# Second-block bursts: two attention groups at a time in four PSUM banks, with every engine in source order

## The chip, the cores and the metric

The kernel runs on one core of one Trainium2 chip. The metric is device time in microseconds (us) for one execution. Five engines work side by side: TensorE (PE in the profile; PEld is its weight loads), VectorE (DVE), ScalarE (ACT), GpSimd (POOL) and SyncE (SP), which here only issues DMAs.

## The reference

Sparse attention over 8 batches, 8 heads, 576 tokens and 64 columns a head, then a two-layer feed-forward with SiLU over all 4608 tokens:

```python
scores = scale * np.matmul(q, k.transpose(0, 1, 3, 2))
mask_local = (rel >= 0) & (rel < stride)                       # heads 0 to 3, stride 32
mask_strided = (rel >= 0) & (pos[None, :] % stride == pos[:, None] % stride)   # heads 4 to 7
scores = np.where(masks[None], scores, -1e9)
attn = softmax(scores)                                         # max taken off, sum + 1e-9
x = np.matmul(attn, v).transpose(0, 2, 1, 3).reshape(B * S, H * D)   # 4608 x 512
h = x @ w_in                                                   # 512 x 2048
g = h * (1.0 / (1.0 + np.exp(-h)))
out = g @ w_out                                                # 2048 x 512
```

## The kernel before

**Feed-forward.** The 4608 tokens are cut into nine blocks of 512 (`k` 0 to 8). A block runs through 16 chunks `fc` of 128 hidden columns. For each chunk `hidden` makes a 128x512 product in one PSUM bank of the ring `ps` (4 banks) with 12 matmuls. Weights and inputs are split into a high and a low part in fp32r, and three of the four products of the parts are kept. `silu` follows: `tanh` on ScalarE, then on VectorE `gate` (th), `g_high` (a cast to ghi) and `g_low` (a subtraction to glo). `output` adds the chunk to the four banks `po` of the block, again with 12 matmuls of 512 columns. In program order TensorE does `hidden(fc)` and then `output(fc-1)`, so that `silu(fc)` has one `output` to finish in. At a block's end `store` scales the four `po` banks on ScalarE and SP writes them out. In the last two chunks `x_high` (ScalarE) and `x_low` (VectorE) split the next block's inputs out of the attention result `xb`.

**Attention.** Each batch has six groups (`NG`), three of the local heads (12 tiles each) and three of the strided heads (8, 8 and 6 tiles), taken in turn: local, strided, local and so on. Group `c` of the list `groups` belongs to batch `c // 6`. The first two batches, and the first block with the loading of the weights, are laid out by a planner of its own (`steps.arrange()`), which also scores groups 12 and 13, takes their peaks, exponentials and sums, and scales them. From the second block on, attention is done in bursts between feed-forward chunks. One call `products(c)` is one burst: TensorE multiplies the weights of group `c` by its values (`values_by_halves`, in the left half of two `ps` banks) and scores group `c + 2` (`scores`, in the right half of the same banks). Then ScalarE copies the values into `xb` (`done_by_halves`; a strided group goes through `sort`), VectorE takes the masked scores' minima (`peak`, 6 instruction pairs for a local group, 8 or 6 for a strided one), ScalarE takes an exponential for each, VectorE divides (`total`, `scale`) and transposes by 32x32 blocks (`turn_by_blocks`: two wide transposes and four narrow ones). A matmul of a burst is plain fp32, and the trace records each as two.

`plan` puts six bursts into each of the blocks 1 to 6, after the chunks 0, 3, 5, 8, 11 and 13. Blocks 7 and 8 have none. One list `due` orders the loads on SP: keys and values of a group in turn. TensorE runs in program order throughout. The other engines do so only until the planner's end (`others.close()`); from there the compiler's scheduler orders them by its own cost model.

```python
    others.enter_context(tc.manual_schedule(engines=OTHERS))
```

Of the kernel before, what the change touches and what calls it, by code (L numbers as in the profile page):

```python
# [13 lines left out]
F32 = mybir.dt.float32  # L14
# [3 lines left out]
AF = mybir.ActivationFunctionType  # L18
# [31 lines left out]
KBUFS = 2  # L50
VBUFS = 2
# [34 lines left out]
NG = len(GROUPS)  # L86
# [112 lines left out]
def sparse_attention_ffn(ctx: ExitStack, tc: tile.TileContext, kqt, vt, w_in, w_out, out):  # L199
    nc = tc.nc  # L200
# [5 lines left out]
    ps = ctx.enter_context(tc.tile_pool(name="ps", bufs=8 - NTT, space=PSUM))  # L206
# [158 lines left out]
    class Attention:  # L365
# [36 lines left out]
        def peak(self):  # L402
            g = self.g
            s_ps = self.halves(self.pss)
            self.sm = att.tile([P, 512], F32, name="sm", bufs=3)
            self.s_sb = self.sm.rearrange("p (c h k) -> p c h k", h=2, k=KW)[:, : g.n]
            s_sb = self.s_sb
            sums = att.tile([P, 4, 4, 2], F32, name="sums", bufs=4)
            self.peaks, self.rsum = peaks, rsum = sums[:, 0, : g.n], sums[:, 1, : g.n]
            self.inv = rsum.unsqueeze(3).broadcast_to([P, g.n, 2, KW])  # L410
            for c in range(g.n):
                for h in range(2):

                    nc.vector.tensor_tensor_reduce(  # L414
                        out=s_sb[:, c, h], in0=s_ps[h][:, c], in1=masks[g.local, g.starts[c]][:, :KW],
                        scale=-SCALE, scalar=BIG, op0=ALU.add, op1=ALU.min,
                        accum_out=peaks[:, c, h : h + 1],
                    )
                    if not self.quick:
                        nc.scalar.activation(  # L420
                            out=s_sb[:, c, h], in_=s_sb[:, c, h], func=AF.Exp,
                            bias=peaks[:, c, h : h + 1], scale=-1.0,
                            accum_out=rsum[:, c, h : h + 1],
                        )

        def below(self):
            peaks = self.peaks.unsqueeze(3).broadcast_to([P, self.g.n, 2, KW])
# [132 lines left out]
    def new_x():  # L560
        return [[None] * NP for _ in range(2)]
# [9 lines left out]
    def x_high(k, x, cc, engine="ACT"):  # L571
        for half, name in zip(x, ("xhi", "xlo")):
            half[cc] = ffn.tile([P, T], F32R, name=name, bufs=XBUFS)
        for src, to in parts(k, cc):
            copy[engine](out=x[0][cc][:, to], in_=src)

    def x_low(k, x, cc):
        for src, to in parts(k, cc):
            nc.vector.tensor_sub(out=x[1][cc][:, to], in0=src, in1=x[0][cc][:, to].bitcast(F32))

    def hidden(fc, x, ccs, ph=None):

        if ph is None:
            ph = ps.tile([P, T], F32, name="ps")
        for cc in ccs:
            for n, (wi, xi) in enumerate(((0, 0), (0, 1), (1, 0))):
                nc.tensor.matmul(  # L587
                    ph, weight(0, wi, fc)[:, cc * P : (cc + 1) * P], x[xi][cc],
                    start=(cc, n) == (0, 0), stop=(cc, n) == (NP - 1, 2),
                )  # L590
        return ph
# [117 lines left out]
    x = new_x()  # L709
# [89 lines left out]
    x1 = new_x()  # L799
# [2 lines left out]
        x_steps(1, x1, cc, x_after + nexts, begin + pace * (NFC - 1))  # L802
    for step in steps.arrange():
        step.act()
    others.close()

    due = [(kind, j) for j in range(2 * NG, len(groups)) for kind in "kv"]
    due = [what for what in due if what not in (("k", 2 * NG), ("k", 2 * NG + 1))]
    scored, weighed = set(range(2 * NG + 2)), set(range(2 * NG))

    def load_due():

        while due:
            kind, j = due[0]
            bufs, load_one, read = (KBUFS, load_qk, scored) if kind == "k" else (
                VBUFS, load_v, weighed)
            if j - bufs not in read:
                return
            load_one(groups[j])
            due.pop(0)  # L820

    def products(c):

        banks = [ps.tile([P, 512], F32, name="ps") for _ in range(2)]
        value, later = groups[c], groups[c + 2] if c + 2 < len(groups) else None
        value.values_by_halves([bank[:, : P * 2] for bank in banks])
        weighed.add(c)
        if later:  # L830
            later.scores([bank[:, P * 2 :] for bank in banks])
            scored.add(c + 2)
        load_due()
        value.done_by_halves()
        if later:
            later.peak()
            later.total()
            later.scale()
            later.turn_by_blocks()

    plan = {}
    for c in range(2 * NG, len(groups)):
        b, at = divmod(c, NG)
        plan[b - 1, (0, 3, 5, 8, 11, 13)[at]] = c

    def between(k, fc):
        if (k, fc) in plan:
            products(plan[k, fc])

    for c in (2 * NG, 2 * NG + 1):  # L850
        groups[c].turn_by_blocks()
    load_due()
    lag = (0, NFC - 1, state["g", NFC - 1])
    po = state["po"]
    x = x1
    for k in range(1, NBLK):
        for fc in range(NFC):
            ph = hidden(fc, x, range(NP))
            new = (k, fc, silu(k, fc, ph))
            output(*lag, po)  # L860
            if fc == 0:
                store(k - 1, po)
                po = [ps_o.tile([P, DM], F32, name="po") for _ in range(NTT)]
            between(k, fc)
            lag = new
            if fc >= NFC - 2 and k + 1 < NBLK:
                if fc == NFC - 2:
                    x1 = new_x()
                for cc in range(NP // 2) if fc == NFC - 2 else range(NP // 2, NP):
                    x_high(k + 1, x1, cc)  # L870
                    x_low(k + 1, x1, cc)
                if fc == NFC - 1:
                    x = x1
    output(*lag, po)
    store(NBLK - 1, po)

# [67 lines left out]
```

## Time and profile before

| what | value |
|---|---|
| runs | 902.83 us median of 3 (901.41 to 903.88) |
| the profiled execution | 902.58 us, its span 900.8 us |
| busy shares | PE 98%, PEld 80%, DVE 56%, ACT 33%, POOL 2% |
| matmuls of 512 columns, recorded | 1728 for `hidden`, 1728 for `output` |
| data moved | 64.59 MB, 72 GB/s on average |

The span begins with the first instruction of the profiled execution and ends with its last. A busy PE in these rows is a modelled span: consecutive matmuls overlap in the records, so that the distance between starts tells their rate, not the duration that stands beside them. PEclk is the granted TensorE clock. In rows of the timeline the first number is the start in the span, the second the duration.

### The profile page before, as it was taken

How to read it: one execution, taken by the hardware profiler on the slowest of the kernel's cores; microseconds unless marked ns; L12 is line 12 of the kernel's file. 1: busy time of each engine (PE TensorE's matmuls, PEld its weight loads, DVE VectorE, ACT ScalarE, POOL GpSimd, SP SyncE). 2: the span in 40 equal slices, each digit the busy share in tenths (PEclk: the TensorE clock that was granted, in tenths of full speed). 3: DMA queues.
4: the chain of work that ended last, by engine and by line, in shares of the span. 5: the costliest groups of instructions: out<-in, count | busy, mean ns of one | idle time of the engine just before them, and what ended most of it. 6: DMA issues, size and time to landing. Idle time of an engine off the chain costs nothing.

```text
span 900.8 us, 17950 instructions
## 1 busy us (share of the span) xinstructions
PE 884.3 (98%) x7297; PEld 717.9 (80%) x7297; DVE 508.5 (56%) x1608; ACT 300.5 (33%) x899; POOL 19.9 (2%) x42
## 2 busy tenths in 40 slices
PE   8999998999999999999999999999999999999998
PEld 6777776788887888788878888887888888888886
DVE  6999678455565565646655565456464433333333
ACT  4768453322522333324332252324322221112111
POOL 5100000000000000000000000000000000000000
PEclk9999999999999999999999999999999999999999
DMA  8976542111311212212221131211300010001001
GB/s 259 312 228 191 167 123 87 47 52 40 115 35 37 71 36 91 60 33 75 84 66 34 50 110 30 60 49 50 100 19 10 1 47 1 1 0 47 1 1 47
DMA packets 37042, 64.59 MB, mean 72 GB/s; under 512 B 2912, under 2 KB 23776, under 8 KB 36960
## 3 DMA queue, kind: packets, MB, share of 16 engines
q1 hardware_dynamic: 36960, 63.45, 22.2%
q8 instruction: 57, 0.93, 0.4%
q14 instruction: 25, 0.20, 0.1%
HBM read 54.00 MB, written 9.44 MB: 70 GB/s over the span
## 4 chain that ended last, share of the span: by engine, by line
PE 76%; DVE 12%; ACT 6%; DMA 3%; SPq 1%; issue 1%; ACTq 0%; DVEq 0%
PE po L633 37%; PE ps L587 34%; ACT sm L420 3%; PE ps L502 3%; DVE pt L469 3%; PE ps L396 2%; DMA stage<-w_out 2%; DMA k<-kqt 1%; DVE th L601 1%; DVE glo L613 1%; DVE sm L444 1%; DVE pt L466 1%; DVE stage L293 1%; ACT xb L542 1%; DVE sm L414 1%
## 5 line engine op out<-in xcount | busy, mean ns | idle before, releaser
L587 PE MATMUL ps<-xhi,w 128*128 128x512 f32 x1152 | 386.2, 395 | 1.8 <-DVE th L601 1.3
L587 PEld LDWEIGHTS ps<-xhi,w 128*128 128x128 f32 x1152 | 216.1, 188 | 49.9 <-DVE th L601 1.5
L601 DVE SCALAR_TENSOR_TENSOR th<-th,ps 128x512 f32<-128x512 f32 (+1 forms) x147 | 99.2, 674 | 226.4 <-ACT th L597 225.5
L597 ACT ACTIVATE th<-ps 128x512 f32<-128x512 f32 (+1 forms) x147 | 86.3, 587 | 419.8 <-PE ps L587 417.1
L587 PE MATMUL ps<-xlo,w 128*128 128x512 f32 x576 | 224.3, 389 | 0.0
L633 PE MATMUL po<-w,ghi 128*128 128x512 f32 x504 | 156.8, 392 | 1.7 <-DVE ghi L609 1.7
L587 PEld LDWEIGHTS ps<-xlo,w 128*128 128x128 f32 x576 | 108.2, 188 | 21.3
L633 PEld LDWEIGHTS po<-w,ghi 128*128 128x128 f32 x504 | 95.2, 189 | 22.2 <-DVE ghi L609 2.1
L613 DVE TENSOR_TENSOR glo<-th,ghi 128x512 fp32r<-128x512 f32 (+1 forms) x147 | 100.1, 681 | 11.2 <-DVE ghi L609 0.5
L633 PE MATMUL po<-w,glo 128*128 128x512 f32 x252 | 99.8, 396 | 1.0 <-DVE glo L613 1.0
L633 PE MATMUL po<-stage,ghi 128*128 128x512 f32 x288 | 89.0, 390 | 0.0
L420 ACT ACTIVATE sm<-sm,sums 128x64 f32<-128x64 f32 x226 | 75.6, 337 | 2.9 <-DVE sums L414 2.3
L633 PE MATMUL po<-v,ghi 128*128 128x512 f32 x216 | 66.6, 390 | 0.0
L609 DVE CAST ghi<-th 128x512 fp32r<-128x512 f32 (+1 forms) x142 | 58.8, 414 | 9.4
L633 PEld LDWEIGHTS po<-stage,ghi 128*128 128x128 f32 x288 | 53.9, 188 | 11.2
L633 PEld LDWEIGHTS po<-w,glo 128*128 128x128 f32 x252 | 47.7, 189 | 14.2 <-DVE glo L613 4.4
L469 DVE STREAM_TRANSPOSE pt<-sm 32x192 f32<-32x192 f32 (+1 forms) x144 | 56.5, 392 | 2.7
L633 PE MATMUL po<-stage,glo 128*128 128x512 f32 x144 | 56.6, 393 | 0.5
L633 PEld LDWEIGHTS po<-v,ghi 128*128 128x128 f32 x216 | 40.5, 188 | 8.5
L633 PE MATMUL po<-k,ghi 128*128 128x512 f32 x144 | 44.3, 389 | 0.0
L414 DVE CUSTOM_DVE_ANT_0 sm<-ps,mask_strided 128x64 f32<-128x64 f32 x176 | 27.2, 220 | 28.3 <-ACT xb L542 28.1
L633 PE MATMUL po<-v,glo 128*128 128x512 f32 x108 | 42.1, 390 | 0.5 <-DVE glo L613 0.5
(84 smaller groups left out, 715.6 us busy)
## 6 DMA issues: line engine op xcount, KB each, us to landing
out<-stage SPq DMA_DIRECT2D x36, 256.0 KB, 2.1
v<-vt SPq DMA_DIRECT2D x21, 384.0 KB, 3.7
k<-kqt SPq DMA_DIRECT2D x14, 512.0 KB, 4.1
stage<-w_out SPq DMA_DIRECT2D x14, 512.0 KB, 4.6
stage<-w_in SPq DMA_DIRECT2D x12, 512.0 KB, 4.4
k<-kqt SPq DMA_DIRECT2D x14, 416.0 KB, 4.8
v<-vt SPq DMA_DIRECT2D x14, 256.0 KB, 2.9
k<-kqt SPq DMA_DIRECT2D x7, 448.0 KB, 4.4
```

The source lines that it names most:

```text
L293: nc.vector.scalar_tensor_tensor(out=upper, in0=upper, scalar=3, in1=lower, op0=ALU.logical_shift_left, op1=ALU.bitwise_or,)
L396: nc.tensor.matmul(self.pss[h][rows, c * KW : (c + 1) * KW], kbd[at, 1, g.q0[t] : g.q0[t] + g.rows], kbd[at, 0, g.k0[t] : g.k0[t] + KW], s ...
L414: nc.vector.tensor_tensor_reduce(out=s_sb[:, c, h], in0=s_ps[h][:, c], in1=masks[g.local, g.starts[c]][:, :KW], scale=-SCALE, scalar=BIG, ...
L420: nc.scalar.activation(out=s_sb[:, c, h], in_=s_sb[:, c, h], func=AF.Exp, bias=peaks[:, c, h : h + 1], scale=-1.0, accum_out=rsum[:, c, h ...
L469: nc.vector.transpose(out=pt[to, r % 2], in_=src[rows, 1 - r % 2])
L502: nc.tensor.matmul(self.pso[p][h * D : (h + 1) * D, i * size : (i + 1) * size], vbd[at, 2 * i + h], moved, start=True, stop=True,)
L587: nc.tensor.matmul(ph, weight(0, wi, fc)[:, cc * P : (cc + 1) * P], x[xi][cc], start=(cc, n) == (0, 0), stop=(cc, n) == (NP - 1, 2),)
L597: nc.scalar.activation(out=th[:, cols], in_=ph[:, cols], func=AF.Tanh, scale=0.5)
L601: nc.vector.scalar_tensor_tensor(out=th[:, cols], in0=th[:, cols], scalar=1.0, in1=ph[:, cols], op0=ALU.add, op1=ALU.mult,)
L609: copy[engine](out=g[0][:, cols], in_=th[:, cols])
L613: nc.vector.tensor_sub(out=g[1][:, cols], in0=th[:, cols], in1=g[0][:, cols].bitcast(F32))
L633: nc.tensor.matmul(po[tt], g[gi][:, cols], weight(1, wi, fc), start=fc == 0 and n == 0, stop=fc == NFC - 1 and n == 2,)
```

## The change

From the second block on, three bursts a block take the place of six, after the chunks 1, 6 and 11. A burst takes two groups, a local and a strided one, and so four `ps` banks, which is the whole ring. Within a burst TensorE scores the later local group first, then multiplies the values of the local and of the strided group, and scores the later strided group last. Right behind the burst comes the `output` of the chunk before it, so the next chunk has a `hidden` and no `output`, and two `hidden` follow each other.

The exponentials are a function of their own now (`weigh`). On ScalarE behind a burst stand the copies of both groups, the six exponentials of the local and the first six of the strided group. The other two of the strided group come behind the next chunk's `tanh`, its division behind that chunk's `silu`, and its transposes behind the `silu` of the chunk after that. The loads are two lists, one for keys and one for values, and each is run as far as its buffers allow. All engines run in program order to the end (`others` isn't closed).

```diff
-    others.close()
...
+    due = {"k": list(range(2 * NG + 2, len(groups))), "v": list(range(2 * NG, len(groups)))}
...
+        for kind, bufs, load_one, read in (
+            ("k", KBUFS, load_qk, scored), ("v", VBUFS, load_v, weighed),
+        ):
+            while due[kind] and due[kind][0] - bufs in read:
+                load_one(groups[due[kind].pop(0)])
...
     def products(c):
-        banks = [ps.tile([P, 512], F32, name="ps") for _ in range(2)]
-        value, later = groups[c], groups[c + 2] if c + 2 < len(groups) else None
-        value.values_by_halves([bank[:, : P * 2] for bank in banks])
...
-            later.scores([bank[:, P * 2 :] for bank in banks])
...
+        pairs = []
+        for i in (c, c + 1):
+            banks = [ps.tile([P, 512], F32, name="ps") for _ in range(2)]
+            left, right = ([bank[:, at : at + 256] for bank in banks] for at in (0, 256))
+            pairs.append((groups[i], left, groups[i + 2] if i + 2 < len(groups) else None, right))
+        for value, left, later, right in pairs:
+            if later and later.g.local:
+                later.scores(right)
+            value.values_by_halves(left)
+            if later and not later.g.local:
+                later.scores(right)
...
+        for value, _, later, _ in pairs:
+            value.done_by_halves()
+            if later:
+                later.peak()
...
-        plan[b - 1, (0, 3, 5, 8, 11, 13)[at]] = c
+        plan[(b - 1) * NFC + (1, 6, 11)[at // 2]] = c
...
+    groups[2 * NG].turn_by_blocks()
+    following[NFC].append(groups[2 * NG + 1].turn_by_blocks)
...
+        ph = hidden(fc, x, range(NP))
+        if fc == NFC - 1 and k + 1 < NBLK:
+            x_split(k + 1, range(NP // 2, NP))
+            x = x1
+        new = (k, fc, silu(k, fc, ph))
+        for act in following[at]:
+            act()
+        if lag:
             output(*lag, po)
...
+        if at in plan:
+            laters = products(plan[at])
+            if laters:
+                local, strided = laters
+                local.weigh()
+                strided.weigh(range(3))
+                normalize(local)
+                local.turn_by_blocks()
+                following[at + 1] += [
+                    lambda s=strided: s.weigh(range(3, s.g.n)), lambda s=strided: normalize(s),
+                ]
+                following[at + 2].append(strided.turn_by_blocks)
+            output(*lag, po)
+            lag = None
```

The order on TensorE in a block's middle. Before, around the burst of one local group; L502 are the values, L396 the scores, L633 is `output`, L587 `hidden`:

```order
L633 MATMUL po<-w_0_758,ghi 128x512
L633 MATMUL po<-w_0_727,glo 128x512
L502 MATMUL ps<-pt,v_77 64x32 x24
L396 MATMUL ps<-k_80 32x64 x24
L587 MATMUL ps<-xhi,w_0_614 128x512
L587 MATMUL ps<-xlo,w_0_614 128x512
```

The same place after the change, where L505 are the values and L636 is `output`:

```order
L636 MATMUL po<-w_0_758,ghi 128x512
L636 MATMUL po<-w_0_727,glo 128x512
L396 MATMUL ps<-k_80 32x64 x24
L505 MATMUL ps<-pt,v_77 64x32 x24
L505 MATMUL ps<-pt,v_77 64x54 x16
L396 MATMUL ps<-k_81 64x64 x12
L636 MATMUL po<-w_0_727,ghi 128x512
```

The strided group's products have moved up next to the local group's, the local scores stand ahead of the values, and `output`, not `hidden`, follows.

The order on ScalarE from one block's `store` (stage) on. Before, with L514 and L542 the copies of a local and a strided group, L420 the exponentials, L597 `tanh` and L575 `x_high`:

```order
L645 ACTIVATE stage<-po 128x512 x4
L514 COPY xb<-ps 128x192 x2
L575 CAST xhi<-xb 128x320
L420 ACTIVATE sm,sums<-sm,sums 128x64 x6
L597 ACTIVATE th<-ps 128x512 x3
L542 COPY xb<-ps 128x12x18 x2
L420 ACTIVATE sm,sums<-sm,sums 128x64 x8
L597 ACTIVATE th<-ps 128x512 x2
```

After, from `store` to the next burst's copies (L517, L545 the copies, L423 the exponentials, L600 `tanh`):

```order
L648 ACTIVATE stage<-po 128x512 x4
L600 ACTIVATE th<-ps 128x512
L517 COPY xb<-ps 128x192 x2
L545 COPY xb<-ps 128x12x18 x2
L423 ACTIVATE sm,sums<-sm,sums 128x64 x12
L600 ACTIVATE th<-ps 128x512
L423 ACTIVATE sm,sums<-sm,sums 128x64 x2
L600 ACTIVATE th<-ps 128x512 x4
L517 COPY xb<-ps 128x192 x2
```

Twelve exponentials in a row now stand ahead of a `tanh`, where six or eight did.

The order on VectorE where block 1 begins, with groups 12 and 13 of the planner in work. Before: L444 is `scale` (128x384 for group 12, 128x512 for group 13), L601, L609 and L613 are `silu` of the first chunk of block 1, L466 and L469 the transposes, L437 the sum of group 13's exponentials:

```order
L444 TENSOR_TENSOR sm<-sm,sums 128x384
L601 SCALAR_TENSOR_TENSOR th<-th,ps 128x512
L466 STREAM_TRANSPOSE pt<-sm 128x192 x2
L609 CAST ghi<-th 128x512
L469 STREAM_TRANSPOSE pt<-sm 32x192 x4
L437 TENSOR_REDUCE sums<-sm 128x8
L613 TENSOR_TENSOR glo<-th,ghi 128x512
```

After (L447 `scale`, L440 the sum, L469 and L472 the transposes, L604, L612 and L616 that `silu`):

```order
L447 TENSOR_TENSOR sm<-sm,sums 128x384
L440 TENSOR_REDUCE sums<-sm 128x8
L443 TENSOR_SCALAR sums<-sums 128x8
L444 RECIPROCAL sums<-sums 128x8
L447 TENSOR_TENSOR sm<-sm,sums 128x512
L469 STREAM_TRANSPOSE pt<-sm 128x192 x2
L472 STREAM_TRANSPOSE pt<-sm 32x192 x4
L604 SCALAR_TENSOR_TENSOR th<-th,ps 128x512
L612 CAST ghi<-th 128x512
L616 TENSOR_TENSOR glo<-th,ghi 128x512
```

The sum and the division of group 13 and all transposes of group 12 now stand ahead of that first `silu`. On ScalarE the exponential of group 13 has moved in the same way from behind the first chunk's `tanh` to ahead of it.

More of the change, by code (lines that the diff above doesn't have):

```diff
@@ L418, in peak, with weigh @@
                     )
[L419 to L424, printed above, removed]
+        def weigh(self, cs=None):
+            for c in range(self.g.n) if cs is None else cs:
+                for h in range(2):
+                    nc.scalar.activation(
+                        out=self.s_sb[:, c, h], in_=self.s_sb[:, c, h], func=AF.Exp,
+                        bias=self.peaks[:, c, h : h + 1], scale=-1.0,
+                        accum_out=self.rsum[:, c, h : h + 1],
+                    )
         def below(self):
@@ L804, in sparse_attention_ffn @@
         step.act()
-    others.close()
-    due = [(kind, j) for j in range(2 * NG, len(groups)) for kind in "kv"]
-    due = [what for what in due if what not in (("k", 2 * NG), ("k", 2 * NG + 1))]
+    due = {"k": list(range(2 * NG + 2, len(groups))), "v": list(range(2 * NG, len(groups)))}
     scored, weighed = set(range(2 * NG + 2)), set(range(2 * NG))
     def load_due():
[L813 to L820, printed above, removed]
@@ L841, in sparse_attention_ffn @@
-    plan = {}
-    for c in range(2 * NG, len(groups)):
-        b, at = divmod(c, NG)
-        plan[b - 1, (0, 3, 5, 8, 11, 13)[at]] = c
[L846 to L851, printed above, removed]
+        for kind, bufs, load_one, read in (
[3 more added lines that the diff above has]
+                load_one(groups[due[kind].pop(0)])
@@ new lines, in products @@
+    def products(c):
+        pairs = []
[9 more added lines that the diff above has]
+                later.scores(right)
+        weighed.update((c, c + 1))
+        scored.update((c + 2, c + 3))
+        load_due()
+        for value, _, later, _ in pairs:
+            value.done_by_halves()
+            if later:
+                later.peak()
+        return [later for _, _, later, _ in pairs if later]
@@ L852, in sparse_attention_ffn, with normalize @@
+    def normalize(group):
+        group.total()
+        group.scale()
+    plan, following = {}, collections.defaultdict(list)
+    for c in range(2 * NG, len(groups), 2):
+        b, at = divmod(c, NG)
+        plan[(b - 1) * NFC + (1, 6, 11)[at // 2]] = c
     load_due()
+    groups[2 * NG].turn_by_blocks()
+    following[NFC].append(groups[2 * NG + 1].turn_by_blocks)
     lag = (0, NFC - 1, state["g", NFC - 1])
@@ L855, in sparse_attention_ffn, with x_split @@
     x = x1
[L856 to L859, printed above, removed]
-            output(*lag, po)
[L861 to L873, printed above, removed]
+    def x_split(k, ccs):
+        for cc in ccs:
+            x_high(k, x1, cc)
+            x_low(k, x1, cc)
+    for at in range(NFC, NBLK * NFC):
+        k, fc = divmod(at, NFC)
+        ph = hidden(fc, x, range(NP))
[6 more added lines that the diff above has]
+        if lag:
+            output(*lag, po)
+        if fc == 0:
+            store(k - 1, po)
+            po = [ps_o.tile([P, DM], F32, name="po") for _ in range(NTT)]
+        lag = new
+        if at in plan:
[12 more added lines that the diff above has]
+            lag = None
+        if fc == NFC - 2 and k + 1 < NBLK:
+            x1 = new_x()
+            x_split(k + 1, range(NP // 2))
     output(*lag, po)
```

9 lines of the change are left out of this document (removed).

## The prediction

> **What bounds the kernel now.** First I read the table of windows, one window a block, with bounds at the first matmul of each block's first `hidden` (columns: window, its length, busy time of PE, PEld, DVE, ACT and POOL with counts, TensorE clock, DMA share, GB/s).
>
> ```profile
> 237.35:334.18 96.83, 96.57 (x849) 78.35 (x848) 55.90 (x191) 32.33 (x121) 0.00 (x0) 1.00 0.20 60
> 527.81:624.65 96.84, 96.58 (x850) 78.35 (x848) 55.59 (x191) 32.39 (x121) 0.00 (x0) 1.00 0.19 60
> 135.15:237.35 102.20, 99.36 (x849) 79.76 (x848) 64.74 (x232) 32.77 (x122) 1.20 (x1) 0.98 0.18 58
> 624.65:719.96 95.31, 95.13 (x769) 77.39 (x768) 48.79 (x147) 27.69 (x93) 0.00 (x0) 1.00 0.11 34
> 719.96:807.00 87.04, 87.04 (x385) 72.07 (x384) 30.77 (x51) 13.21 (x22) 0.00 (x0) 1.00 0.03 13
> ```
>
> The first two rows are the first and last of four equal blocks (2 to 5). Then come block 1, block 6 and block 7, which has no attention. PE has next to no idle time in any block but block 1, so TensorE bounds the part that changes. Block 7 is 32 pieces (`hidden` or `output`) in 87.04, which is 2.72 a piece and 0.227 a matmul. So attention costs a full block 96.83 - 87.04 = 9.79 us of TensorE's time.
>
> Next the timeline of TensorE shows what a burst costs, a strided one at 260.93 and a local one at 273.61 (start, duration, engine, line).
>
> ```profile
> 260.93 0.69 PE L502 MATMUL ps<-pt,v 64*64 64x54 f32 x32
> 261.44 0.66 PE L396 MATMUL ps<-k 64*64 64x64 f32 x32
> 262.03 0.50 PE L587 MATMUL ps<-xhi,w 128*128 128x512 f32 x1
> ...
> 270.33 0.61 PE L633 MATMUL po<-w,ghi 128*128 128x512 f32 x2
> 271.12 0.50 PE L633 MATMUL po<-w,glo 128*128 128x512 f32 x1 [0.17 <-DVE glo L613]
> ...
> 273.30 0.39 PE L633 MATMUL po<-w,glo 128*128 128x512 f32 x1
> 273.61 0.90 PE L502 MATMUL ps<-pt,v 64*64 64x32 f32 x48
> 274.44 0.72 PE L396 MATMUL ps<-k 64*32 64x64 f32 x48
> 275.10 0.50 PE L587 MATMUL ps<-xhi,w 128*128 128x512 f32 x1
> ...
> 277.97 0.62 PE L633 MATMUL po<-w,ghi 128*128 128x512 f32 x2
> ```
>
> From start to start: local values 0.83, local scores 0.66, strided values 0.51, strided scores 0.59. Going in costs 0.31 - 0.227 = 0.08, say 0.09. Coming out, the next piece takes 277.97 - 275.10 = 2.87 for 2.72, so 0.15. A switch in and out is thus 0.24, whatever is inside. The row at 271.12 is a wait: glo comes 0.34 late (0.79 after the row before it, where two matmuls take 0.45).
>
> A block's bursts: three local ones at 0.24 + 0.83 + 0.66 = 1.73; strided ones of 8 tiles at 0.24 + 0.51 + 0.59 = 1.34, less 0.12 each where the values or the scores have 6 tiles (three quarters of 0.51 and 0.59): 3.78. Sum 5.19 + 3.78 = 8.97. The block pays 9.79, so 0.82 of waits on VectorE are in it, of which the row at 271.12 is one.
>
> **The change in blocks 2 to 5.** Three switches for six: 3 x 0.24 = 0.72 less. The small products stay: 3 x 1.49 + 3.06 = 7.53. If nothing waits, a block is 87.04 + 7.53 + 0.72 = 95.29, a gain of 1.54, or 6.1 for four blocks. Whether nothing waits is the question, since behind a burst ScalarE and VectorE have both groups' work. Rows of the two engines for the same bursts:
>
> ```profile
> 262.14 0.97 ACT L542 COPY xb<-ps 128x216 f32<-128x216 f32 x2 [3.23 <-PE ps L396]
> 263.01 0.35 ACT L420 ACTIVATE sm<-sm,sums 128x64 f32<-128x64 f32 x1
> ...
> 265.58 0.19 ACT L420 ACTIVATION_READ_ACCUMULATOR sm<-sm,sums 128x1 f32 x1
> 265.67 0.58 ACT L597 ACTIVATE th<-ps 128x512 f32<-128x512 f32 x1
> 270.53 0.60 ACT L597 ACTIVATE th<-ps 128x512 f32<-128x512 f32 x1 [4.28 <-PE ps L587]
> 275.19 0.54 ACT L514 COPY xb<-ps 128x192 f32<-128x192 f32 x2 [4.06 <-PE ps L396]
> 275.81 0.35 ACT L420 ACTIVATE sm<-sm,sums 128x64 f32<-128x64 f32 x1
> ```
>
> ```profile
> 262.74 0.22 DVE L414 CUSTOM_DVE_ANT_0 sm<-ps,mask_strided 128x64 f32<-128x64 f32 x1 [1.77 <-ACT xb L542]
> 263.76 0.22 DVE L414 CUSTOM_DVE_ANT_0 sm<-ps,mask_strided 128x64 f32<-128x64 f32 x1
> ...
> 271.16 0.69 DVE L601 SCALAR_TENSOR_TENSOR th<-th,ps 128x512 f32<-128x512 f32 x1
> 271.95 0.43 DVE L609 CAST ghi<-th 128x512 fp32r<-128x512 f32 x1
> 272.49 0.69 DVE L613 TENSOR_TENSOR glo<-th,ghi 128x512 fp32r<-128x512 f32 x1
> ...
> 277.94 0.17 DVE L440 TENSOR_SCALAR sums<-sums 128x6 f32<-128x6 f32 x1 [1.45 <-ACT sm L420]
> 278.38 0.56 DVE L444 TENSOR_TENSOR sm<-sm,sums 128x384 f32<-128x384 f32 x1
> 278.97 0.64 DVE L466 STREAM_TRANSPOSE pt<-sm 128x192 f32<-128x192 f32 x2
> ...
> 281.19 0.69 DVE L601 SCALAR_TENSOR_TENSOR th<-th,ps 128x512 f32<-128x512 f32 x1
> ```
>
> To be read: eight exponentials take 265.67 - 263.01 = 2.66, 0.333 each. The peaks of a bank begin when ScalarE's copy of it ends (262.74) and are 0.145 apart. A local group's division and transposes take 281.19 - 277.94 = 3.25, and begin 277.94 - 275.81 = 2.13 after its first exponential. A `silu` runs tanh 0.63, gate 0.79, cast 0.54, subtraction 0.69: ghi is there 1.85 after its `tanh` starts, glo 2.65 after.
>
> Now a new burst, its clock at 0 where the next large matmul would have started. TensorE: in 0.09, local scores to 0.75, local values to 1.58, strided values to 2.09, strided scores to 2.68; `output(fc)` 2.87 to 5.55; `hidden(fc+1)` to 8.27; `hidden(fc+2)` to 10.99; then `output(fc+1)`, which wants ghi at 10.99 and glo 0.45 later, at 11.44. ScalarE: local copies 0.1 after TensorE has gone on to the next group (275.19 against 275.10), at 1.68; strided copies likewise at 2.78; exponentials 0.87 later (263.01 against 262.14), at 3.65, twelve of them to 7.65. A tanh can start 0.2 after its `hidden`'s piece (138.07 below, where the piece ended at 135.15 + 2.72), here at 8.47, and finds ScalarE free. VectorE: local peaks from the first copy's end, 2.0 to 3.0, strided peaks likewise to 4.9; the local division at 3.65 + 2.13 = 5.78, the transposes done at 9.03; the gate can start at 8.47 + 0.63 = 9.10. So ghi comes at 10.32 and glo at 11.12: both in time, with 0.3 to spare on glo, but only 0.07 in VectorE's queue ahead of the gate. The strided rest (two exponentials, 1.1 of division, 2.6 of transposes) then has three chunks. A strided group of three copies instead of two shifts ScalarE by some 0.3 and eats the slack, once a block. I take no wait. Ends for what the trace can't show (four kinds of small products in a row, a queue in source order): a gain of the waits alone at best, 0 more; at worst another switch of 0.24 a burst, 18 x 0.24 = 4.3.
>
> Ring of four: the burst's fourth bank is that of `hidden(fc)`, whose gate must have read it. That gate ends 0.2 + 0.63 + 0.69 = 1.5 after `hidden(fc)`, during `output(fc-1)`, and the bank is written 2.72 + 1.6 after it. `hidden(fc+1)` needs the local banks read: at 3.0, wanted at 5.55. Nothing waits.
>
> Loads in lists of their own: SP issues the keys when a burst's scores are done, the values behind them. The next burst is five chunks, some 27 us, away.
>
> ```profile
> v<-vt SPq DMA_DIRECT2D x21, 384.0 KB, 3.7
> ```
>
> They are hidden by that, as they were; a late one would hold a burst one for one. `x_high` and `x_low` of a block's last chunk and the four `store` copies stand ahead of a `tanh` now, but fall into `output` and `hidden` pieces in which both engines are free. I cost them at nothing, and with them goes the second wait in the 0.82.
>
> **Block 6** has two later groups fewer. It saves 0.72 and one wait like that at 271.12, some 0.4 with its slower restart: 1.1.
>
> **Block 1** is dearer than its neighbours by 102.20 - 96.83 = 5.4. The rows:
>
> ```profile
> 153.84 0.73 PE L633 MATMUL po<-w,ghi 128*128 128x512 f32 x2 [1.66 <-DVE ghi L609]
> 154.60:158.00 3.40, 3.40 (x8) 2.73 (x9) 1.62 (x3) 0.00 (x0) 0.00 (x0) 0.50 0.00 0
> ...
> 138.07 0.60 ACT L597 ACTIVATE th<-ps 128x512 f32<-128x512 f32 x1 [3.47 <-PE ps L587]
> 140.41 0.63 ACT L432 ACTIVATE sm<-sm 128x512 f32<-128x512 f32 x1 [0.24 <-POOL sm L428]
> 139.18 1.20 POOL L428 TENSOR_TENSOR sm<-sums,sm 128x512 f32<-128x512 f32 x1 [8.45 <-DVE sums L414]
> 142.57 0.69 DVE L437 TENSOR_REDUCE sums<-sm 128x8 f32<-128x512 f32 x1
> 144.21 0.69 DVE L444 TENSOR_TENSOR sm<-sm,sums 128x512 f32<-128x512 f32 x1
> 144.93 0.77 DVE L466 STREAM_TRANSPOSE pt<-sm 128x256 f32<-128x256 f32 x2
> ```
>
> TensorE stands 1.66 for ghi, and then the granted clock is 0.50 for 3.4 us, which loses 1.7 more. The new order removes that place and makes another. ScalarE must do group 13's exponential, which waits for POOL until 140.38, before the first chunk's tanh (138.07 before). VectorE then sums from 141.04 (0.69), divides (0.44 + 0.72) and transposes group 12 (3.25 - 1.03 = 2.22), so the gate starts at 145.1, ghi is there at 146.3, glo at 147.1. TensorE: `hidden` of the first chunk from 135.15, `output` to 140.59, `hidden` of the second to 143.31, and then it stands for 3.0, with glo 0.3 more. Two `x_low` pieces of block 2 leave VectorE's queue ahead of group 13's peaks, which gives back some 0.3 (estimate, by the size of the narrow pieces): a stall of 3.0. Behind it the burst finds its transposes done. Block 1 is then 95.29 + 3.0 = 98.3, and if the stall halves the clock once more, 100.0: a gain of 2.2 with, 3.9 without. I take the halving, since an idle of 1.66 was followed by one. [...]
>
> **Sum.** 6.1 + 1.1 + 2.2 = 9.4 off the profiled execution's 902.58 (its span 900.8 and 1.8 around it; the median of the runs shown is 902.83): 893.2. Blocks 0, 7 and 8 and the tail keep TensorE's order and are left as they are.
>
> **Rivals.**
> Small waits remain at each burst: VectorE's 0.07 is used up and glo comes 0.1 to 0.4 late, 18 times, 2 to 7 us: 895 to 900. For it: the slack; against it: the 0.3 on glo.
> Slower: the twelve exponentials hold the `tanh` behind them. Before, the wait at 265.67 was already of that kind (its `hidden`, begun at 262.03, had let go at 262.03 + 2.87 + 0.2 = 265.1). If each cost its 0.35 and its 0.19 of accumulator read one after the other, they would end at 3.65 + 6.5 = 10.1, the tanh 1.7 late, and TensorE would lose 1.4 a burst (0.3 is spare): 25 us, 918. It decides from 9.4 / 18 = 0.52 a burst on. Against it: the pitch of 0.333 in the rows. [...]
> No change: TensorE's gain is real, but waits of 0.4 to 0.6 a burst take its place; 900 to 905.
> Better: block 1's stall doesn't come (the exponential of group 13 earlier than 140.4) and the clock stays: 3 + 1.7 less, 888.5 to 890.
>
> **How the numbers follow.** Forecast with or without the halving, 890 to 895: 0.55, its own range. Small waits: 0.22. Slower: 0.07. No change: 0.08. Better: 0.08. The range 889.5 to 899 leaves out the slower case, no change, and a part of the better. A measurement here can tell 0.3%, 2.7 us, from no change: faster 0.85, same 0.08, slower 0.07.
>
> **What would show it.** Blocks 2 to 5 at 95.3 each; three switches of 0.24 a block; no wait of `output` on glo or ghi two chunks behind a burst; tanh of the chunk behind the burst starting with its `hidden`'s end; one stall near 143 of about 3 us on ghi, with or without a halved clock behind. The prediction is wrong if blocks 2 to 5 stay above 96.3, or if block 1's stall is far from 3.

## Result and profile after

| | before | after |
|---|---|---|
| median of the runs beside each other, us | 902.37 | 894.01 (892.20 to 895.09) |
| ratio, 95% interval | | 0.9905 (0.9886 to 0.9925) |
| profiled execution, its span | 902.58, 900.8 | 893.06, 891.2 |
| block 0 and what lies ahead of it | 135.15 | 137.24 |
| block 1 | 102.20 | 99.98 |
| blocks 2 to 5, each | 96.83 | 94.84 |
| block 6 | 95.31 | 93.74 |
| block 7 | 87.04 | 87.04 |

The table of windows of the kernel after, one window a block as before (blocks 1, 2 and 6):

```profile
137.24:237.22 99.98, 97.26 (x849) 79.31 (x848) 67.16 (x231) 31.77 (x122) 1.20 (x1) 0.98 0.20 65
237.22:332.06 94.84, 94.84 (x849) 78.47 (x848) 56.93 (x190) 31.70 (x121) 0.00 (x0) 1.00 0.19 61
616.58:710.32 93.74, 93.74 (x770) 77.44 (x768) 48.35 (x144) 27.09 (x93) 0.00 (x0) 1.00 0.10 34
```

In blocks 2 to 6 PE's busy time equals the length of the window: no wait is left. The gains are 4 x 1.99 there, 1.57 in block 6 and 2.22 in block 1, together 11.75. The head takes 2.09 back, which leaves 9.6 between the spans. The head isn't the change: in all 13 profiled executions of this study its order is that of before (up to its last few steps), and block 1 began at 134.5 to 137.7, with 136.0 in the middle. This execution of after had a slow head.

A burst in block 3, on TensorE, then on ScalarE and VectorE (start, duration, engine, line):

```profile
343.04 0.72 PE L396 MATMUL ps<-k 64*32 64x64 f32 x48
343.69 1.39 PE L505 MATMUL ps<-pt,v 64*64 64x32 f32 x80
344.90 0.66 PE L396 MATMUL ps<-k 64*64 64x64 f32 x32
345.48 0.73 PE L636 MATMUL po<-w,ghi 128*128 128x512 f32 x2
...
348.36 0.39 PE L590 MATMUL ps<-xhi,w 128*128 128x512 f32 x1
...
353.80 0.62 PE L636 MATMUL po<-w,ghi 128*128 128x512 f32 x2
354.25 0.39 PE L636 MATMUL po<-w,glo 128*128 128x512 f32 x1
```

```profile
351.28 0.60 ACT L600 ACTIVATE th<-ps 128x512 f32<-128x512 f32 x1 [0.84 <-PE ps L590]
...
350.17 1.52 DVE L472 STREAM_TRANSPOSE pt<-sm 32x192 f32<-32x192 f32 x4
351.91 0.69 DVE L604 SCALAR_TENSOR_TENSOR th<-th,ps 128x512 f32<-128x512 f32 x1 [0.22 <-ACT th L600]
352.63 0.43 DVE L612 CAST ghi<-th 128x512 fp32r<-128x512 f32 x1
353.09 0.69 DVE L616 TENSOR_TENSOR glo<-th,ghi 128x512 fp32r<-128x512 f32 x1
```

From start to start: local scores 0.65, both groups' values 1.21 in one run, strided scores 0.58. ScalarE has idled 0.84 when the `tanh` comes, VectorE 0.22 when the gate comes. ghi is done at 353.06 and wanted at 353.80; glo is done at 353.78 and wanted at 354.25.

The start of block 1, on ScalarE, VectorE and TensorE, and two neighbouring windows of 3.41:

```profile
142.22 0.63 ACT L435 ACTIVATE sm<-sm 128x512 f32<-128x512 f32 x1 [5.93 <-POOL sm L431]
142.75 0.58 ACT L600 ACTIVATE th<-ps 128x512 f32<-128x512 f32 x1
...
142.88 0.69 DVE L440 TENSOR_REDUCE sums<-sm 128x8 f32<-128x512 f32 x1 [1.60 <-ACT sm L435]
...
145.32 1.52 DVE L472 STREAM_TRANSPOSE pt<-sm 32x192 f32<-32x192 f32 x4
146.87 0.69 DVE L604 SCALAR_TENSOR_TENSOR th<-th,ps 128x512 f32<-128x512 f32 x1
...
148.23 0.70 PE L636 MATMUL po<-w,ghi 128*128 128x512 f32 x2 [2.67 <-DVE ghi L612]
...
145.93:149.34 3.41, 1.11 (x4) 0.66 (x5) 3.14 (x8) 0.26 (x1) 0.00 (x0) 1.00 0.42 162
149.34:152.75 3.41, 3.41 (x10) 2.50 (x8) 3.08 (x7) 0.00 (x0) 0.00 (x0) 0.50 0.00 0
```

Group 13's exponential waits for GpSimd, ahead of the first `tanh`; group 13's sum and group 12's transposes stand ahead of the first gate. TensorE stands 2.67, and the second window has half the clock. From start to start, `hidden` takes 5.55 instead of 2.72, which is 2.83 more, and the `output` behind it 4.77 instead of 2.72, which is 2.05 more. The half clock is not all of the 2.05: in the kernel of experiment 5 the same stall, 5.56 by this measure, was not followed by half a clock, and that `output` still took 3.19. So 1.58 is the half clock, and the other 0.47 is, by the rows of that run, glo that comes late (0.71 behind the first ghi matmul for 0.45), the restart (0.12 more in the next four matmuls) and the way into the burst (0.09).

### The profile page after: what moved, and what is told of

It is laid out like the page before. It is cut to its first block, busy times and chain, and to the rows that moved or that the text cites. A ratio compares the mean times of both kernels' runs of the same rounds, so it can differ in the third digit from the quotient of the medians.

```text
span 891.2 us, 17991 instructions
## 1 busy us (share of the span) xinstructions
PE 875.1 (98%) x7297; PEld 718.4 (81%) x7297; DVE 516.4 (58%) x1608; ACT 296.4 (33%) x899; POOL 20.4 (2%) x42
## 4 chain that ended last, share of the span: by engine, by line
PE 88%; DVE 5%; DMA 4%; ACT 2%; issue 1%; SPq 0%; POOLq 0%; ACTq 0%; DVEq 0%
PE po L636 41%; PE ps L590 40%; PE ps L396 3%; PE ps L505 3%; DMA stage<-w_out 2%; DMA stage<-w_in 1%; DVE stage L293 1%; DVE w L337 1%; DVE th L604 1%; PE ps L707 1%; DVE sm L414 0%; ACT stage L282 0%; ACT stage L287 0%; DMA k<-kqt 0%; DVE glo L616 0%
## 5 line engine op out<-in xcount | busy, mean ns | idle before, releaser
L590 PE MATMUL ps<-xhi,w 128*128 128x512 f32 x1152 | 378.2, 390 | 2.8 <-DVE th L604 1.7
L604 DVE SCALAR_TENSOR_TENSOR th<-th,ps 128x512 f32<-128x512 f32 (+1 forms) x147 | 99.3, 675 | 266.0 <-ACT th L600 265.9
L600 ACT ACTIVATE th<-ps 128x512 f32<-128x512 f32 (+1 forms) x147 | 86.5, 589 | 448.3 <-PE ps L590 447.0
L636 PE MATMUL po<-w,ghi 128*128 128x512 f32 x504 | 158.6, 396 | 2.8 <-DVE ghi L612 2.7
L636 PEld LDWEIGHTS po<-w,ghi 128*128 128x128 f32 x504 | 93.9, 189 | 23.8 <-issue 3.5
L616 DVE TENSOR_TENSOR glo<-th,ghi 128x512 fp32r<-128x512 f32 (+1 forms) x147 | 100.1, 681 | 12.3 <-DVE ghi L612 0.5
L636 PE MATMUL po<-w,glo 128*128 128x512 f32 x252 | 98.9, 393 | 0.0
L636 PE MATMUL po<-stage,ghi 128*128 128x512 f32 x288 | 88.9, 390 | 0.0
L423 ACT ACTIVATE sm<-sm,sums 128x64 f32<-128x64 f32 x226 | 75.1, 340 | 0.0
L636 PE MATMUL po<-v,ghi 128*128 128x512 f32 x216 | 67.4, 393 | 0.0
L612 DVE CAST ghi<-th 128x512 fp32r<-128x512 f32 (+1 forms) x142 | 60.0, 423 | 11.8
L636 PEld LDWEIGHTS po<-stage,ghi 128*128 128x128 f32 x288 | 53.9, 188 | 11.3
L472 DVE STREAM_TRANSPOSE pt<-sm 32x192 f32<-32x192 f32 (+1 forms) x144 | 56.5, 392 | 2.6
L636 PEld LDWEIGHTS po<-w,glo 128*128 128x128 f32 x252 | 47.7, 189 | 11.0 <-DVE glo L616 0.9
L636 PE MATMUL po<-stage,glo 128*128 128x512 f32 x144 | 56.0, 389 | 0.0
L636 PEld LDWEIGHTS po<-v,ghi 128*128 128x128 f32 x216 | 40.0, 188 | 8.5
L636 PE MATMUL po<-k,ghi 128*128 128x512 f32 x144 | 44.3, 389 | 0.0
L423 ACT ACTIVATION_READ_ACCUMULATOR sm<-sm,sums 128x1 f32 x226 | 44.0, 195 | 0.0
L636 PE MATMUL po<-v,glo 128*128 128x512 f32 x108 | 42.1, 390 | 0.7 <-DVE glo L616 0.7
```

The source lines that it names most:

```text
L423: nc.scalar.activation(out=self.s_sb[:, c, h], in_=self.s_sb[:, c, h], func=AF.Exp, bias=self.peaks[:, c, h : h + 1], scale=-1.0, accum_ou ...
L472: nc.vector.transpose(out=pt[to, r % 2], in_=src[rows, 1 - r % 2])
L590: nc.tensor.matmul(ph, weight(0, wi, fc)[:, cc * P : (cc + 1) * P], x[xi][cc], start=(cc, n) == (0, 0), stop=(cc, n) == (NP - 1, 2),)
L600: nc.scalar.activation(out=th[:, cols], in_=ph[:, cols], func=AF.Tanh, scale=0.5)
L604: nc.vector.scalar_tensor_tensor(out=th[:, cols], in0=th[:, cols], scalar=1.0, in1=ph[:, cols], op0=ALU.add, op1=ALU.mult,)
L612: copy[engine](out=g[0][:, cols], in_=th[:, cols])
```

## The experiments

Times are medians, ratios are to the kernel before on the same chip.

**1. Source order alone.** The kernel before, less one line:

```diff
-    others.close()
```

> The kernel before with one part of the change alone: every engine in source order to the end; six bursts of one group a block and one load list as before. Theory (source order takes the waits of 0.82 a block away, pairing takes the switches and drains): blocks 2 to 5 at 96.0 (87.04 + 8.97) for 96.83. Rival (pairing takes the waits away; source order alone leaves or adds waits): blocks 2 to 5 at 96.8 or more. In both, block 1 grows by a stall of 5 to 6 us, since group 13's division and the transposes of both groups stand ahead of the first silu: 104 to 106 with a halved clock. Time by the theory 901 to 903, by the rival 905 to 908.

Measured: 909.5, ratio 1.0074 (1.0050 to 1.0098), slower than before. Block 2's window, and behind a strided burst VectorE and TensorE:

```profile
239.66:337.42 97.76, 97.17 (x850) 78.07 (x849) 57.57 (x191) 32.21 (x121) 0.00 (x0) 1.00 0.19 60
...
270.23 1.78 DVE L469 STREAM_TRANSPOSE pt<-sm 32x256 f32<-32x256 f32 x4
272.04 0.69 DVE L601 SCALAR_TENSOR_TENSOR th<-th,ps 128x512 f32<-128x512 f32 x1
...
273.25 0.73 PE L633 MATMUL po<-w,ghi 128*128 128x512 f32 x2 [0.37 <-DVE ghi L609]
```

The rival is right: source order alone adds waits. Where the later strided group has 8 tiles, all of its transposes stand ahead of the gate, `hidden` takes 3.25 for 2.72 and `output` 3.21 for 2.81, and a block has two such places: some 1.8 on 96.0. Block 1 is at 104.35, as expected; the time lies 1.5 above the rival's range.

**2. Pairs, but scheduled.** The changed kernel with that line put back behind the planner:

> The changed kernel, but ScalarE, VectorE and SP go back to the compiler's scheduler at the planner's end; TensorE keeps the order of the changed kernel (bursts of two groups). Theory (source order is needed, the slack behind a burst is only 0.2 to 0.7 us): the scheduler puts a part of the strided group's rest ahead of a gate, and blocks 2 to 5 come to 95.3 to 97. Rival (pairing alone does it): blocks 2 to 5 at 94.84 as in the changed kernel, no wait behind a burst. Block 1 may lose its stall in either case, since the scheduler can let the first silu pass. Time by the theory 894 to 902, by the rival 889 to 894.

Measured: 977.18, ratio 1.0822 (1.0795 to 1.0850), far outside both expectations. A block's window, and the place behind a burst:

```profile
362.67:472.45 109.78, 100.08 (x849) 80.82 (x848) 56.82 (x191) 32.09 (x121) 0.00 (x0) 0.95 0.16 53
...
382.14 0.57 ACT L600 ACTIVATE th<-ps 128x512 f32<-128x512 f32 x1
...
384.55 1.78 DVE L472 STREAM_TRANSPOSE pt<-sm 32x256 f32<-32x256 f32 x4
386.36 0.69 DVE L604 SCALAR_TENSOR_TENSOR th<-th,ps 128x512 f32<-128x512 f32 x1
...
387.56 0.74 PE L636 MATMUL po<-w,ghi 128*128 128x512 f32 x2 [3.01 <-DVE ghi L612]
```

The `tanh` is early enough, but the scheduler puts the division and the transposes of both groups ahead of the gate. TensorE's order is the same as in the changed kernel. So the 894 rest on what stands ahead of the gate on VectorE, and I had that effect too small by a factor of seven or so (2 a block at most, 15 measured, the halved clocks among them).

**3. How much may stand ahead of the gate.** Two doses on the changed kernel: the strided group's division ahead of the next `silu`, then its transposes as well.

```diff
-                strided.weigh(range(3))
+                strided.weigh()
...
-                following[at + 1] += [
-                    lambda s=strided: s.weigh(range(3, s.g.n)), lambda s=strided: normalize(s),
-                ]
-                following[at + 2].append(strided.turn_by_blocks)
+                normalize(strided)
+                strided.turn_by_blocks()      # in the second dose only; else as before
```

> The changed kernel, but the last two exponentials and the division of the strided group stand ahead of the next chunk's tanh and silu (the transposes stay two chunks behind). Theory, with the slack as the changed kernel's rows show it (VectorE idle 0.22 ahead of the gate, ghi done 0.74 before it is wanted): the gate starts 0.83 later, ghi comes 0.15 late and glo 0.25 more, 0.4 a burst, less behind a 6-tile group: blocks 2 to 5 at 95.7 to 96.1, time about 899 to 900. Rival 1 (the slack as the prediction had it, 0.07 and 0.3): 0.7 a burst, blocks at 96.9, time about 905. Rival 2 (VectorE isn't near the limit): blocks at 94.84, time 894.

> As the run with the division ahead, and the strided group's transposes stand ahead of the next chunk's silu too, so that all of both groups is done before it. The gate then starts 3.4 later and TensorE stands some 2.7 for ghi and 0.2 for glo behind each of 17 bursts. Theory 1 (a stall of 1.7 us or more halves the clock once each time, 1.7 to 2.05 lost): blocks 2 to 5 at 94.84 + 3 x 2.9 + 3 x 1.9 = 109, time about 975. Theory 2 (the clock is judged in stretches of 3.41 us on a fixed grid, and halves only after one that was idle for about half or more; a stall of 2.7 that falls on both sides of a grid line needn't do it): a part of the stalls halves the clock, blocks between 103.5 and 109 and unequal among themselves, time 945 to 970. [...]

Measured: the first 899.61, ratio 0.9964 (0.9946 to 0.9983); the second 964.33 in one run. Windows of block 2 in the first dose, then of blocks 2 and 5 in the second:

```profile
237.42:333.61 96.19, 96.18 (x849) 78.01 (x848) 57.14 (x190) 31.71 (x121) 0.00 (x0) 1.00 0.18 61
```

```profile
245.48:354.17 108.69, 101.23 (x850) 81.45 (x848) 57.44 (x190) 31.71 (x121) 0.00 (x0) 0.95 0.17 54
571.93:678.59 106.66, 99.20 (x850) 80.12 (x848) 57.49 (x190) 31.71 (x121) 0.00 (x0) 0.97 0.17 55
```

The first dose costs (96.2 - 94.84) / 3 = 0.45 a burst, by the theory 0.4: the slack read from the rows is close to the true one, the block is 0.1 above the theory's range, and the time is as expected. The second costs 11.8 to 14.1 a block, stalls and halved clocks together. Its blocks differ, as theory 2 has it: in block 2 all three stalls were followed by half the clock, in block 5 two.

**4. Six bursts, put off.** The kernel of experiment 1 with the strided rest put off as the changed kernel has it.

```diff
-            later.total()
-            later.scale()
-            later.turn_by_blocks()
+            acts = [later.total, later.scale, later.turn_by_blocks]
...                                            # a local group at once, a strided one:
+                following[at + 1] += acts[:2]
+                following[at + 2] += acts[2:]
```

> Six bursts of one group a block and one load list as before, every engine in source order, and the division of a strided group behind the next chunk's silu, its transposes behind the silu after that, as the changed kernel has it. What is left between this and the changed kernel in blocks 2 to 5 is the pairing alone. Theory (in source order the waits of 1.8 a block come from the strided rest ahead of a gate, and pairing saves three switches of 0.24 and three drains of 0.13 to 0.15): blocks 2 to 5 at 96.0, which is 1.17 above the changed kernel. Rival (pairing also takes waits away, or costs some): blocks 2 to 5 at 96.4 or more. Block 1 is as in the run with source order alone, 104 to 105; time about 901.

Measured: 909.68 in one run, for about 901, and blocks at 98.0 to 98.4. The theory's 96.0 is missed; the rival's 96.4 or more has come, but by a wait that neither of them names. The waits behind the bursts are gone (but for one of 0.27 in block 2), and another has come, at the block's start:

```profile
532.11:630.14 98.03, 96.31 (x850) 78.31 (x848) 57.22 (x191) 32.10 (x121) 0.00 (x0) 1.00 0.19 60
...
241.16 0.50 PE L587 MATMUL ps<-xlo,w 128*128 128x512 f32 x1 [1.72 <-DVE xlo L579]
```

The last burst of a block stands after chunk 13 there, so its put-off rest is ahead of the second half of `x_low`, which follows the `silu` of chunk 15, and the first `hidden` of the next block takes 4.75 for 2.72. Less these 2.03 the block is at 96.0, as the theory has it. In the changed kernel the last burst stands after chunk 11, so its rest is done by then, and the second half of the split stands ahead of the `silu` of chunk 15; which of the two it takes was not tried. Pairing alone is thus worth 1.2 a block, 0.72 of it the switches; the places of the bursts and of the split of x belong to the change.

**5. Each group by itself in the burst.**

```diff
-            if later and later.g.local:
-                later.scores(right)
             value.values_by_halves(left)
-            if later and not later.g.local:
+            if later:
                 later.scores(right)
```

> The changed kernel with another order inside a burst: local values, local scores, strided values, strided scores, so that the values of the two groups don't follow each other. Theory (the 0.45 a block by which the changed kernel beat the forecast of 95.29 is the drain between the two groups' values and their neighbours, which falls away where the values run on): 0.13 a burst more, blocks 2 to 5 at 95.23, time 2.3 more than the changed kernel, about 896. Rival (the 0.45 is waits or a cheaper switch, not the order of the products): blocks at 94.84, time 894.

Measured: 894.74, ratio 0.9916 (0.9883 to 0.9949), too close to the changed kernel to be told from it by time (the profiled execution lost nothing to a halved clock); the blocks tell it. A block's window and a burst:

```profile
234.98:330.27 95.29, 95.29 (x849) 78.75 (x848) 56.97 (x190) 31.68 (x121) 0.00 (x0) 1.00 0.19 61
...
341.25 0.90 PE L505 MATMUL ps<-pt,v 64*64 64x32 f32 x48
342.08 0.72 PE L396 MATMUL ps<-k 64*32 64x64 f32 x48
342.73 0.69 PE L505 MATMUL ps<-pt,v 64*64 64x54 f32 x32
343.24 0.66 PE L396 MATMUL ps<-k 64*64 64x64 f32 x32
343.82 0.50 PE L636 MATMUL po<-w,ghi 128*128 128x512 f32 x1
```

The block is at 95.29, the prediction's very number. Values that run on cost 1.21 for 0.83 + 0.51, so 0.13 a burst is what the changed order saves. The starts of single records say where that lies (medians of blocks 2 to 5 in both runs). From the last record of one product to the first of the next it takes 0.146 to 0.149 where the tile, the figure behind the names in these rows, changes between 64*64 and 64*32. It takes 0.038 where the tile stays 64*64, for values behind values and for scores behind values alike. The changed order has one change of tile fewer among a burst's small products, and that is 0.11 of the 0.13. Why a change of tile has this price, no run shows.

**6. The load lists.** First the old list, keys and values in turn (`due` and its loop as before the change), then one list in the order of the pairs:

```diff
+    due = [(kind, j) for i in range(2 * NG, len(groups), 2) for kind in "kv" for j in (i, i + 1)]
...                                            # the loop of one list, as before the change
```

> The changed kernel with the load list of before: keys and values in turn in one list. Theory (a load lands 27 us or so ahead of its burst either way): blocks 2 to 5 at 94.84, time within 0.2% of the changed kernel, 893 to 895. Rival (the lists of their own matter; values would be held up behind keys): a burst waits for its values, blocks 2 to 5 at 95.5 or more, time 897 or more.

> The changed kernel with one load list again, but in the order of the pairs: the keys of two groups, then the values of two groups. Every load is issued before its burst. Theory (loads land long before their burst, the lists carry no time): blocks 2 to 5 at 94.84, time as the changed kernel's, 892 to 895. Rival (keys first in a list of their own is worth something): blocks 2 to 5 at 95.3 or more, time 896 or more.

Measured: 891.46, ratio 0.9868 (0.9838 to 0.9898), and 892.96, ratio 0.9889 (0.9867 to 0.9911); blocks 2 to 5 at 94.84 in both. The first says nothing on lateness, and its time is not that of a kernel that does the work: in the old order the keys of the strided group stand behind values that only the same burst releases, so its scores read the keys of two groups earlier, don't wait, and the output is wrong. What it shows is that pairs can't be fed from that list. In the second every load stands ahead of its burst, and the time is that of the changed kernel: lists of their own carry no time.

**7. Block 1 without its stall.** The exponential, sum and division of group 13 and both groups' transposes go behind the first two `silu`, and the first burst one chunk later. Then two more: the first burst in its place, with all of that work behind the first `silu` alone; and the first burst two chunks later, else as the first of the three.

```diff
+        if last == "U":
+            return
...
-    attention_steps(2 * NG + 1, (late[1], late[1] + 8, 0, 0), "S")
+    attention_steps(2 * NG + 1, (late[1], late[1] + 8, 0, 0), "U")
...
-    groups[2 * NG].turn_by_blocks()
-    following[NFC].append(groups[2 * NG + 1].turn_by_blocks)
+    soon, then = groups[2 * NG], groups[2 * NG + 1]
+    following[NFC] += [soon.turn_by_blocks, then.exp]
+    following[NFC + 1] += [lambda: normalize(then), then.turn_by_blocks]
...
-        plan[(b - 1) * NFC + (1, 6, 11)[at // 2]] = c
+        plan[(b - 1) * NFC + (1, 6, 11)[at // 2] + (c == 2 * NG)] = c    # 0 * and 2 * (...) in the others
```

> Starts from the changed kernel; only block 1's beginning differs: group 13's exponential, sum and division and the transposes of group 12 stand behind the first chunk's silu instead of ahead of it, and the first burst comes one chunk later (after chunk 2). Theory (the stall of 2.83 us is work of groups 12 and 13 in front of the first gate on VectorE, and the 2.05 us of half clock follow from the stall): block 1 falls from 99.98 to about 95.1, no halved clock, no wait of output in block 1; time about 889 (894.0 less 4.9), ratio to before about 0.985. Rival 1 (the work doesn't fit and the stall only moves to the burst or the output behind it): block 1 stays at 98 to 100, time 892 to 894. Rival 2 (the halved clock has nothing to do with the stall): block 1 at 97.1 with one halved stretch, time 891.

> As the run with the first chunk free, but the first burst stands after chunk 1 as in the changed kernel, and behind the first silu VectorE does all that is left of groups 12 and 13 at once (transposes of 12, sum and division of 13, transposes of 13). Theory (of the 2.07 that block 1 was still above its neighbours there, 1.5 was a wait of TensorE in the strided scores for nothing that the profile names, which goes with the place of the burst in TensorE's instructions): VectorE is done at 150.3 for strided values wanted at 150.0, so a wait of 0.3, and 0.3 to 0.5 at the second burst as in the changed kernel: block 1 at 95.4 to 95.8, time about 887.5. Rival 1 (that wait belongs to the loads issued behind the local scores, wherever the burst stands): block 1 at 97, time 889. Rival 2 (VectorE's pile of 6.7 us behind the first silu holds the burst and the output behind it by more than 1): block 1 at 97 or more, waits on pt or ghi.

> As the run with the first chunk free, but the first burst one chunk later again (after chunk 3). It asks what the 2.0 us are by which block 1 stays above its neighbours in both runs without the stall: there TensorE waits in or behind the first two bursts (1.5 and 0.55; 1.04 and 0.91) for nothing that the profile names, though the operands are there. Theory (TensorE's supply of instructions runs dry where a burst's many short instructions follow soon on block 0; a packet of the instruction queue ends 1.3 to 1.6 us ahead of the resumption in one of these runs): with another chunk of long products ahead, the wait in the first burst moves or shrinks, block 1 at 95.4 to 96.2, time 887.5 to 888.3. Rival (the wait belongs to the first burst, to its loads or its groups, wherever it stands): block 1 at 96.9, time 889, the wait in the strided scores as in the run with the first chunk free.

Measured: after chunk 2 888.97, ratio 0.9847 (0.9821 to 0.9873); after chunk 1 888.81, ratio 0.9852 (0.9828 to 0.9876); after chunk 3 886.82, ratio 0.9821 (0.9801 to 0.9841), the fastest of all. Block 1 of the three in this order, the first burst of the first run, and that of the second with the gate on VectorE:

```profile
137.66:234.57 96.91, 95.47 (x849) 78.59 (x848) 67.14 (x231) 31.87 (x122) 1.20 (x1) 1.00 0.21 68
...
136.29:233.17 96.88, 95.31 (x849) 78.65 (x848) 66.90 (x231) 31.87 (x122) 1.20 (x1) 1.00 0.20 68
...
134.76:230.06 95.30, 95.12 (x850) 78.40 (x849) 67.15 (x231) 31.89 (x122) 1.20 (x1) 1.00 0.21 69
```

```profile
155.93 0.65 PE L396 MATMUL ps<-k 64*64 64x64 f32 x28
157.76 0.33 PE L396 MATMUL ps<-k 64*64 64x64 f32 x4 [1.18 <-issue]
158.02 0.74 PE L636 MATMUL po<-w,ghi 128*128 128x512 f32 x2
```

```profile
149.76 0.61 PE L505 MATMUL ps<-pt,v 64*64 64x54 f32 x26 [0.82 <-DVE th L604]
...
149.02 0.69 DVE L604 SCALAR_TENSOR_TENSOR th<-th,ps 128x512 f32<-128x512 f32 x1
```

With the work of groups 12 and 13 behind the first gate neither the stall nor the half clock comes. Two of the three blocks stay 2.0 above their neighbours all the same, so the time of the first is the expected one and its block 1 is not. They have waits in or behind the first two bursts (1.5 and 0.55, 1.04 and 0.91).

The 1.04 of the second run has a name. The strided values go into the two last banks of the ring, of which the fourth is that of the chunk's `hidden`; after their first four records TensorE stands until the gate that reads this bank ends at 149.71. The gate stands behind the pile on VectorE, so this is the mechanism of that run's rival 2.

The 1.5 of the first run lies in the strided scores, whose operands are there, and the profile puts it down to "issue". After chunk 3 it is gone, and 0.46 is left at the second burst. One thing in the traces speaks for a supply of instructions that runs dry. Counted in TensorE's records (weight loads, matmuls and semaphore instructions), the wait at the second burst begins at the same record, the 4034th, in all ten kernels with pairs, wherever the bursts stand, and the 1.5 begins at the 3522nd, 512 earlier. TensorE goes on 1.3 to 1.5 us after the end of a packet of 16384 bytes on the DMA queue that the profile calls "instruction". No run changed that supply, so the cause is argued and not shown.

## Why the prediction was right, and where it wasn't

The time came out (893.2 forecast; 894.01 the median, 893.06 the profiled execution), in part because errors cancel: blocks 2 to 6 gave 2.3 more than forecast, and the head of that execution was 2.1 longer than the one the sum was made against.

**Blocks 2 to 5**, 95.29 forecast, 94.84 measured. The mis-sized term is the small products, 7.53: they were added up as 0.83 + 0.51 and so on from bursts of one group, where another change of tile follows the local values, though the changed order has none there. Three times 0.13 is 0.39 of the 0.45; the same burst without the run-on gave 95.29. The switch of 0.24 held (in 0.09, `output` 2.85 to 2.89). Block 6's 1.57 for 1.1 has some of it too: without the run-on in the first two bursts it is at 94.01 for 93.74 (experiment 5). The rest of that gap was not taken apart.

**No wait behind a burst** in blocks 2 to 6: right, and the rival of small waits with it wrong. The slack was a little larger than forecast: 0.22 in VectorE's queue for 0.07, 0.74 on ghi for 0.67, 0.47 on glo for 0.3. Experiment 3 shows it is real and how it ends: 1.05 more work ahead of the gate costs 0.45 a burst, 3.6 more costs 4 to 5. The twelve exponentials end 0.84 ahead of the `tanh`, so the slower rival was far off. The gain rests on this margin, which the prediction put at 0.07: where the scheduler's order takes it away (experiment 2), the time is 83 higher.

**Block 1**, 100.0 forecast, 99.98 measured: the stall and the late glo behind it were 2.83 + 0.38 for 3.0, the half clock cost 1.58 for 1.7, the rest of the block was 0.45 less, and 0.3 came at the second burst, which the prediction did not have. That the stall had that cause experiment 7 shows. That it halves the clock was taken from one case, and came true by luck: in experiment 5 the same stall, at the same place, didn't.

**Loads, store, split of x**: costed at nothing, and nothing they were. That the split costs nothing hangs on where it and the last burst stand (experiment 4).

## What the runs showed of the clock

In the traces of before and after the stretch at 0.50 in block 1 begins a multiple of 3.413 us behind the start of the first full one (44 of them before, 41 after): the clock changed on a grid here, and by the rows below what counted is how much of one stretch TensorE idled. The same stall in the run with each group by itself, its two stretches; then from the second dose of experiment 3 a stall of 2.76 across a grid line, with the stretch behind it, and a stall of 2.18 inside one:

```profile
142.76:146.17 3.41, 1.55 (x7) 0.94 (x5) 3.27 (x9) 1.88 (x4) 0.00 (x0) 1.00 0.80 308
146.17:149.59 3.42, 2.61 (x10) 1.91 (x11) 3.12 (x8) 0.00 (x0) 0.00 (x0) 1.00 0.00 0
```

```profile
596.58 0.73 PE L636 MATMUL po<-w,ghi 128*128 128x512 f32 x2 [2.76 <-DVE ghi L612]
...
591.72:595.13 3.41, 2.10 (x10) 1.40 (x8) 3.23 (x9) 0.61 (x2) 0.00 (x0) 1.00 0.00 0
595.13:598.55 3.42, 1.98 (x7) 1.35 (x8) 3.11 (x7) 0.00 (x0) 0.00 (x0) 1.00 0.00 0
598.55:601.96 3.41, 3.41 (x16) 2.81 (x15) 0.62 (x1) 0.00 (x0) 0.00 (x0) 1.00 0.02 5
...
625.85:629.27 3.42, 1.24 (x6) 0.74 (x5) 3.25 (x9) 0.60 (x1) 0.00 (x0) 1.00 0.00 0
629.27:632.68 3.41, 3.41 (x9) 2.46 (x9) 2.19 (x4) 0.00 (x0) 0.00 (x0) 0.50 0.02 5
```

The 2.76 are cut into 1.31 and 1.44, and the clock stays; the 2.18 lie in one stretch, and it falls. So, by what TensorE idled in one stretch: behind 2.30 (after) and 2.18 the clock fell, behind 1.31 and 1.44 it stayed, and in between both came: the kernel before idled 1.66 in its stretch (151.19 to 154.60) and lost the clock, the first window above idled 1.86 and kept it. Of 18 stalls in the second dose 15 halved it, and its granted clock was 0.972 on average. The grid lies differently against the span's start from trace to trace: a stretch begins at 154.60 before, at 149.34 after and at 146.17 in the run with each group by itself, and no two of these are a multiple of 3.413 apart. Single stalls of 1.66 (before) and 2.67 (after) were followed by half the clock.

Where the clock fell, the `output` behind such a stall took 4.77 (block 1 of after); where it stayed, 3.19 (block 1 of experiment 5) and 3.12 (the second dose, behind the 2.76). So one kernel with one stall of this size may gain or lose some 1.6 us from one execution to the next, an estimate from these two sizes. The four runs of experiment 5's kernel rank the same way: 892.95 at a granted clock of 1.000, 894.61 and 894.87 at 0.998 and 0.996, 897.83 at 0.994.

## What to carry to other kernels

Before a burst is made larger, list what stands in each engine's queue ahead of the one instruction that the bound engine waits for next, and put off all of the rest; here that was worth more than the switches saved, and the margin was read from the trace to 0.2 us. Add up small products only in the order in which they will run, since a change of tile between them had its own price, 0.11 here. A stall of 1.66 to 2.76 on the bound engine cost its own length here and, by luck, another 1.6 us or nothing. Removing the last such stall took 3.1 to 4.7 us off its block here, and 5 to 7 us off the medians.
